# Chunk attention and a Mish feed-forward on one core: 72 transfers issued by GpSimd in place of SyncE

## The chip, the cores and the metric

The kernel runs on one core of a Trainium2 chip. The core has a matrix engine (TensorE, "PE" in the profile; its weight loads are shown apart as "PEld"), a vector engine (VectorE, "DVE"), an activation engine (ScalarE, "ACT"), GpSimd ("POOL") and SyncE ("SP"), which here issues transfers only. "SPq", "ACTq" and so on are the sequencers of these engines: what they do there (issue a transfer, wait for a semaphore) is not counted as busy time. Every engine works through its own list of instructions in order. Transfers run on 16 DMA engines that all issuing engines share.

The metric is the time of one execution on the device in microseconds (us); lower is better.

## What is computed

Inputs are q, k and v of shape 8 x 8 x 576 x 64 in float32 and two float64 weight matrices, `w_in` (512 x 2048) and `w_out` (2048 x 512).

```python
# attention in chunks of 64 positions, every head on its own
scores = q_c @ k_c.T / 8                 # 64 x 64 for each chunk
attn = softmax(scores)
x = (attn @ v_c)                         # as 4608 tokens x 512
# feed-forward
h = x @ w_in
g = h * tanh(softplus(h))                # Mish
out = g @ w_out
```

The result is 4608 x 512 in float32. The matrix products are made from float32 values split into an upper and a lower part, with three matmuls for each product.

## The kernel before

**Work and stages.** The tokens are worked on in 18 pairs of 256 tokens. Pairs 0 and 1 form the first block; the other 16 make four blocks of four pairs. While a block goes through the feed-forward, the attention of the next one is made beside it.

- *First block* (0 to about 138 us). It does three things at once: attention and feed-forward of pairs 0 and 1; the unpacking of the float64 weights, piece by piece (`w_load`, L102, loads a piece into the tile `wst`; `w_scale`, `w_bits`, `w_hi` and `w_lo` turn it into upper and lower parts in `wi` and `wo`; `w_bits` also stores `w_in`'s whole values to `cs` in DRAM, L136); and attention of pairs 2 to 5. The order of all steps on all engines is written out by hand in the string `ORDER`, and nothing is reordered afterwards (`tc.manual_schedule()`). Two pieces of weights fit into `wst`, so a load waits until `w_bits` is done with the piece two before it. `w_keep` ("keep", L169 and L170) stores `w_in`'s parts to `wa` in DRAM.
- *Blocks 1 and 2* (about 138 to 503 us). The product with `w_in` is made with seven half-size products in place of eight (`product`, L756), for which sums and differences of quarter blocks of the weights and of x are needed. A block takes eight steps `unit(m, u)`, each of seven products in the order of `PRODUCTS`, and then `phase_two(m)`. A product's weight operand is a tile `w` of 256 KB, loaded by `load_op` (L743) from `wa`; the load is put in the list five products ahead of its use. The first blocks of weights (A11, A12, A22) were stored by `w_keep`, the sums (S1 to S4) by `s_lo`.
- *Blocks 3 and 4* (about 503 to 838.8 us). Both products are made with seven half-size ones (`up_two`, `down_all`); `load_op` also loads from `wb`, where `t_keep` and `t_lo` put the parts of `w_out` and its sums.

**The sums of weights.** For each of eight parts u of `w_in`, `s_load(u)` (L184) loads the whole values from `cs` into the tile `a`; `s_adds` (L196, VectorE) makes four sums; `s_hi` (L200, ScalarE) and `s_lo` (L204, VectorE) split them; `s_lo` then stores them to `wa` (L207). There is one buffer for `a`, so `s_load(u + 1)` waits for that store to land. Parts 0 and 1 start in the first block, and part u is made during unit u - 1 of block 1, at the places in `S_PLACES`. For `w_out`, `t_whole`, `t_sums`, `t_hi` and `t_lo` do the same from `wo`, without a load, during block 2, and `t_lo` stores to `wb` (L237).

**q, k and v.** `load_qk` (L261) loads q and k of a pair and `load_v` (L269) its v, 512 KB each. Pairs 0 and 1 are loaded at the very start, into tiles named `q`, `k` and `room`. In the first block the pairs 2 to 5 take a tile `qk` from the pool `xo` of seven buffers, which also serves the two `room` tiles, the weights `wi` and the parts of x; later pairs take two buffers of the pool `at` (three buffers, shared with `p`, `ps` and `v`) or of `ob`. In the ORDER string the loads of the later pairs stand between steps of the weights, for example

```
... load 0, scale 0, ..., a_T 1 1, a_copy 1 1, a_V 1 1, load_qk 0, scores 0, ...
... hi 18, lo 18, s_load 0, inverse 3, x 0 8, up 14, fill 13, fill 14, norm 3, keep 5, load_v 3, keep 7, ...
... s_hi 0, s_lo 0, s_load 1, x 0 6, T 3, up 15, copy 3, ops 3, gl 14, fill 15, V 3, ...
```

(`load_qk 0` is pair 2, `load_v 3` pair 5.) In block 1 and 2 a unit loads v for the pair whose scores it makes and q and k for the next pair (`unit`, L816 to L841).

**Queues.** Nearly all transfers are issued by SyncE, in the order in which the steps are listed. An issue that has to wait for a semaphore (a buffer, data, or the landing of a transfer eight places back) holds all that follow on that engine. ScalarE issues two of the first loads of k and some of the last stores. GpSimd issues none: it sets four constants and the identity matrix at the start and has no further work.

Of the kernel before, what the change touches and what calls it, by code (L numbers as in the profile page):

```python
# [23 lines left out]
def kernel(  # L24
# [22 lines left out]
    nc = tc.nc  # L47
# [11 lines left out]
    at = ctx.enter_context(tc.tile_pool(name="at", bufs=3))  # L59
# [19 lines left out]
    ops_of = [dram.tile([P, 7, 2, 256], F32, name=f"wa_{u}") for u in range(NU)]  # L79
    ops_out = [dram.tile([P, 7, 2, 256], F32, name=f"wb_{u}") for u in range(NU)]  # L80
# [100 lines left out]
    def s_load(u):  # L181
        if u < NU:
            bld["t"] = c_p.tile([P, 4, 2, 256], F32, name=f"a_{u}", tag="c")
            nc.sync.dma_start(  # L184
                out=bld["t"][:, :, 1], in_=w_c[u].rearrange("p h (a c) -> p (h a) c", a=2)
            )

# [14 lines left out]
    def s_lo(u):  # L202
        t = bld["t"]
        nc.vector.tensor_tensor(  # L204
            out=t[:, :, 1].bitcast(F32R), in0=t[:, :, 1], in1=t[:, :, 0], op=ALU.subtract
        )
        nc.sync.dma_start(out=ops_of[u][:, 3:], in_=t)  # L207


    def t_whole(u):  # L210
# [21 lines left out]
    def t_lo(u):  # L232
        t = bld["o"]
        nc.vector.tensor_tensor(
            out=t[:, :, 1].bitcast(F32R), in0=t[:, :, 1], in1=t[:, :, 0], op=ALU.subtract
        )
        nc.sync.dma_start(out=ops_out[u][:, 3:], in_=t)  # L237

    def t_keep(u):
        for n, (f, a) in enumerate(((0, 0), (1, 0), (1, 1))):  # L240
# [6 lines left out]
    st = {}  # L247
    BOTH = slice(0, 2)

    def load_qk(j, qk=None, ts=(BOTH,), queues=(nc.sync, nc.sync), pool=(at, "A")):  # L250
        if qk is None:
            if pool[0] is xo_p:
                both = xo_p.tile([P, 2, 2, H, CHUNK], F32, name=f"qk_{j}", tag="x")
                qk = [both[:, 0], both[:, 1]]
            else:
                qk = [
                    pool[0].tile([P, 2, H, CHUNK], F32, name=f"{n}_{j}", tag=pool[1]) for n in "qk"
                ]
        for t in ts:
            for x, src, queue in zip(qk, (q, k), queues):  # L260
                queue.dma_start(  # L261
                    out=x[:, t], in_=src[2 * j : 2 * j + 2][t].rearrange("t p h c -> p t h c")
                )
        st[j] = {"q": qk[0], "k": qk[1]}

    def load_v(j, vs=None):
        if vs is None:
            vs = at.tile([P, 2, H, D], F32, name=f"v_{j}", tag="A")
        nc.sync.dma_start(out=vs, in_=v[2 * j : 2 * j + 2].rearrange("t p h c -> p t h c"))  # L269
        st[j]["v"] = vs  # L270

    def small_mm(o, l, r, ts):
# [126 lines left out]
    def first_pair(m):  # L399
        return PAIRS + 4 * (m - 1)  # L400
# [58 lines left out]
    def up(i, cols=slice(0, TOK), last="x"):  # L459
        x = xs["first"]  # L460
        if i not in it:
            it[i] = {"h": ps_h.tile([P, TOK], F32, name=f"h_{i}", tag="h")}
        h = it[i]["h"]
        n = 0
        parts = ((1, 0), (0, 0), (0, 1))
        for w_, x_ in parts if last == "x" else reversed(parts):
            for kt in range(NK):
                nc.tensor.matmul(  # L468
                    h[:, cols],
                    lhsT=wi[i // 2][:, i % 2 * 2 + kt // 2, w_, kt % 2],  # L470
                    rhs=x[:, x_, kt, cols],
                    start=(n == 0),
                    stop=(n == 3 * NK - 1),
                )
                n += 1
# [86 lines left out]
    FIRST, SECOND = slice(0, 1), slice(1, 2)  # L562
# [6 lines left out]
    A, B = slice(0, PTOK), slice(PTOK, TOK)  # L569
# [6 lines left out]
    def room(n):  # L576
        if n not in rooms:
            rooms[n] = xo_p.tile([P, 2, 2, H, CHUNK], F32, name=f"room_{n}", tag="x")
        return rooms[n]

    def open_accumulators():
        first.close()
        opened["o"] = ctx.enter_context(tc.tile_pool(name="ps_o", bufs=1, space=bass.MemoryType.PSUM))

    TOP = {
        "qk0": lambda: load_qk(0, None, (FIRST, SECOND), (nc.sync, nc.scalar)),
        "v0": lambda: load_v(0, room(0)[:, 0]),
        "qk1": lambda: load_qk(1, (room(0)[:, 1], room(1)[:, 0]), (FIRST, SECOND)),
        "v1": lambda: load_v(1, room(1)[:, 1]),
        "up0A": lambda: up(0, A),  # L590
        "up0B": lambda: up(0, B),
        "up1": lambda: up(1, last="w"),
# [52 lines left out]
    def atom(name, *args):  # L645
# [9 lines left out]
        elif name in steps:  # L655
            steps[name](a)
        elif name in attention:
            attention[name](j)
        elif name == "up":
            up(a, last="w")  # L660
        elif name == "gh":
            g_upper(it[a], it[a]["z"], f"0_{a}", a in BY_SCALAR)
        elif name == "gl":
            g_lower(it[a], it[a]["z"], f"0_{a}")
        elif name == "fill":
            if a < NF - 1:
                filled()
            down(0, a, it[a])
        elif name == "mish":
            it[a]["z"] = z_tile(f"z_{a}")  # L670
            mish(it[a]["z"], it[a]["h"])
        elif name == "keep":
            w_keep(a)
        elif name == "x":
            x_step(1, *args)
        elif name == "ops":
            for _ in range(a):
                load_op()
        else:
            {"s_load": s_load, "s_adds": s_adds, "s_hi": s_hi, "s_lo": s_lo}[name](a)  # L680

    attention = {
        "scores": a_scores,
        "load_v": load_v,
        "max": a_max,
        "sub": a_sub,
# [5 lines left out]
        "V": a_values,  # L692
        "raw": a_raw,
        "load_qk": lambda j: load_qk(j, pool=(xo_p, "x")),
    }

# [72 lines left out]

    zb = {}  # L770
    S_STEPS = (s_adds, s_adds, s_hi, s_lo, s_load)
    S_PLACES = ((1, 1, 1, 3, 5), (0, 3, 3, 4, 6), (2, 2, 4, 4, 6))
    X_LATE = ((9, 0), (10, 4), (6, 2), (8, 0))
# [8 lines left out]

    BUILDS_OUT = {}
    T_STEPS = (t_whole, t_sums, t_hi, t_lo)
    for n in range(NU):
        for i, step in enumerate(T_STEPS if n < NU - 1 else ()):
# [420 lines left out]
    with tc.manual_schedule():  # L1207
# [6 lines left out]
        p = first_pair(BOTH_FROM - 1)  # L1214
# [53 lines left out]
```

## Time and profile before

| | |
|---|---|
| Time, median of 3 runs | 843.26 us (843.57, 840.75, 843.26) |
| Time of the profiled execution | 840.62 us |
| Its span, first to last instruction | 838.8 us |
| TensorE busy | 804.2 us (96%) |
| VectorE, ScalarE, GpSimd busy | 529.9, 437.6 and 0.7 us |
| Bytes on the queue of SyncE | 179.60 MB, of 181.38 MB in all |
| Mean granted TensorE clock | 0.993 of full speed |

In rows of the profile, "L756 PE MATMUL x<-x_T,w" is line 756, the engine, the operation, and the tile written from the tiles read. In a list in order of time the first two numbers are start and duration in us, and "[2.56 <-DMA v<-in_v]" says that the engine stood idle for 2.56 us before and that the landing of v ended it. In a list of waits the three numbers are us in total, times, and the longest. "DMA wst<-in_w_in" in the chain of work that ended last is a transfer, from issue to landing. In the page's list of issues the last number is the median us from issue to landing. TensorE's clock is a share of full speed.

### The profile page before, as it was taken

How to read it: one execution, taken by the hardware profiler on the slowest of the kernel's cores; microseconds unless marked ns; L12 is line 12 of the kernel's file. 1: busy time of each engine (PE TensorE's matmuls, PEld its weight loads, DVE VectorE, ACT ScalarE, POOL GpSimd, SP SyncE). 2: the span in 40 equal slices, each digit the busy share in tenths (PEclk: the TensorE clock that was granted, in tenths of full speed). 3: DMA queues.
4: the chain of work that ended last, by engine and by line, in shares of the span. 5: the costliest groups of instructions: out<-in, count | busy, mean ns of one | idle time of the engine just before them, and what ended most of it. 6: DMA issues, size and time to landing. Idle time of an engine off the chain costs nothing.

```text
span 838.8 us, 15546 instructions
## 1 busy us (share of the span) xinstructions
PE 804.2 (96%) x6088; PEld 673.5 (80%) x6088; DVE 529.9 (63%) x797; ACT 437.6 (52%) x649; POOL 0.7 (0%) x6
## 2 busy tenths in 40 slices
PE   4889988899999999999999999999999999999998
PEld 3668776688888887788888888787899988888887
DVE  5988997646465654576574844554798723348875
ACT  4788884444354444354444535555656524445443
POOL 0000000000000000000000000000000000000000
PEclk9999999999999999999999999999999999999999
DMA  8799957875876403888876129876567786666763
GB/s 285 258 326 307 322 198 262 301 264 193 281 254 202 126 1 113 277 264 276 285 247 210 39 101 310 278 229 180 160 182 207 208 238 194 191 193 177 213 194 104
DMA packets 92280, 181.38 MB, mean 216 GB/s; under 512 B 9008, under 2 KB 23344, under 8 KB 90160
## 3 DMA queue, kind: packets, MB, share of 16 engines
q1 hardware_dynamic: 91600, 179.60, 67.7%
q8 instruction: 49, 0.80, 0.4%
q10 hardware_dynamic: 608, 0.79, 0.3%
q14 instruction: 23, 0.19, 0.1%
HBM read 137.36 MB, written 42.99 MB: 215 GB/s over the span
## 4 chain that ended last, share of the span: by engine, by line
PE 73%; DVE 10%; DMA 8%; ACT 5%; issue 2%; SPq 1%; DVEq 0%; ACTq 0%
PE x L756 17%; PE v L756 9%; PE y L756 5%; PE X L1115 4%; DMA wst<-in_w_in 4%; PE Z L1115 3%; PE Z L1067 3%; PE X L1067 2%; PE X_a L1067 2%; DVE wc L132 2%; PE av L278 2%; PE s L278 2%; PE Y L1067 1%; PE o_(1, 1)_0_2753 L506 1%; PE o_(2, 1)_0_4405 L506 1%
## 5 line engine op out<-in xcount | busy, mean ns | idle before, releaser
L756 PE MATMUL x<-x_T,w 128*128 128x512 f32 x576 | 144.6, 395 | 1.9 <-ACT G L1001 1.1
L756 PEld LDWEIGHTS x<-x_T,w 128*128 128x128 f32 x576 | 107.1, 189 | 27.4 <-ACT G L1001 2.8
L1021 ACT CAST gh<-G 128x512 fp32r<-128x512 f32 x96 | 59.1, 621 | 58.2 <-PE X_a L1067 16.3
L1023 DVE TENSOR_TENSOR gl<-G,gh 128x512 fp32r<-128x512 f32 x96 | 65.4, 690 | 29.3 <-ACT gh L1021 28.4
L481 ACT ACTIVATE G<-G 128x512 f32<-128x512 f32 x48 | 30.3, 632 | 57.4 <-DVE G L768 57.4
L768 DVE TENSOR_TENSOR G<-v,G 128x512 f32<-128x512 f32 x32 | 21.9, 690 | 57.1 <-ACT G L1001 34.7
L468 PE MATMUL h<-x_first,wi 128*128 128x512 f32 (+1 forms) x204 | 47.6, 383 | 4.1 <-ACT z L481 3.0
L756 PE MATMUL v<-x_T,w 128*128 128x512 f32 x192 | 48.0, 393 | 2.1 <-DMA w<-wa 2.1
L756 PE MATMUL y<-x_B,w 128*128 128x512 f32 x192 | 49.0, 398 | 0.3 <-DMA w<-wa 0.3
L481 ACT ACTIVATE zb<-zb 128x512 f32<-128x512 f32 x32 | 20.2, 632 | 55.6 <-DVE zb L768 55.5
L756 PE MATMUL v<-x_B,w 128*128 128x512 f32 x192 | 48.5, 393 | 0.0
L756 PE MATMUL x<-x_B,w 128*128 128x512 f32 x192 | 48.2, 393 | 0.0
L468 PEld LDWEIGHTS h<-x_first,wi 128*128 128x128 f32 x204 | 36.1, 188 | 12.9 <-ACT z L481 3.8
L756 PEld LDWEIGHTS v<-x_T,w 128*128 128x128 f32 x192 | 36.0, 188 | 10.2 <-DVE a L196 2.5
L492 DVE CAST gh<-z 128x512 fp32r<-128x512 f32 x39 | 16.5, 424 | 41.0 <-PE o_(2, 0)_3_3320 L506 20.6
L756 PEld LDWEIGHTS v<-x_B,w 128*128 128x128 f32 x192 | 35.7, 188 | 7.9 <-DVE zb L768 0.4
L506 PE MATMUL o<-wo,gh 128*128 128x512 f32 x128 | 40.7, 398 | 1.0 <-DVE wo L160 1.0
L756 PEld LDWEIGHTS y<-x_B,w 128*128 128x128 f32 x192 | 35.1, 188 | 8.0 <-issue 0.4
L756 PEld LDWEIGHTS x<-x_B,w 128*128 128x128 f32 x192 | 35.4, 188 | 7.1 <-issue 0.2
L1115 PE MATMUL X<-w,gh 128*128 128x256 f32 x256 | 36.0, 284 | 0.0
L496 DVE TENSOR_TENSOR gl<-z,gh 128x512 fp32r<-128x512 f32 x48 | 32.9, 690 | 1.3
L1115 PEld LDWEIGHTS X<-w,gh 128*128 128x128 f32 x256 | 33.1, 192 | 0.1
(211 smaller groups left out, 1673.4 us busy)
## 6 DMA issues: line engine op xcount, KB each, us to landing
w<-wa SPq DMA_DIRECT2D x224, 256.0 KB, 3.2
w<-wb SPq DMA_DIRECT2D x112, 256.0 KB, 2.9
v<-in_v SPq DMA_DIRECT2D x16, 512.0 KB, 5.8
wa<-a SPq DMA_DIRECT2D x8, 1024.0 KB, 4.9
wb<-t SPq DMA_DIRECT2D x8, 1024.0 KB, 5.0
wst<-in_w_out SPq DMA_DIRECT2D x7, 1024.0 KB, 7.1
wst<-in_w_in SPq DMA_DIRECT2D x6, 1024.0 KB, 7.9
q<-in_q SPq DMA_DIRECT2D x12, 512.0 KB, 4.3
```

The source lines that it names most:

```text
L132: nc.vector.scalar_tensor_tensor(out=c, in0=x, scalar=mask, in1=y, op0=op, op1=ALU.bitwise_or)
L278: nc.tensor.matmul(o[h * CHUNK : (h + 1) * CHUNK, c, t - ts.start, g], lhsT=l[rows, t, 2 * g + h], rhs=r[rows, t, 2 * g + h], start=True, ...
L468: nc.tensor.matmul(h[:, cols], lhsT=wi[i // 2][:, i % 2 * 2 + kt // 2, w_, kt % 2], rhs=x[:, x_, kt, cols], start=(n == 0), stop=(n == 3 * ...
L481: nc.scalar.activation(out=out_, in_=in_, func=AF.Mish)
L496: nc.vector.tensor_tensor(out=d["gl"], in0=z, in1=d["gh"].bitcast(F32), op=ALU.subtract)
L506: nc.tensor.matmul(acc[t], lhsT=g[:, t * P : (t + 1) * P], rhs=wo[:, f, part], start=(f == 0 and n == 0), stop=(f == NF - 1 and n == 2),)
L756: nc.tensor.matmul(o, lhsT=t[:, w_, kt], rhs=x[x_][:, kt], start=(start and i == 0), stop=(i == 5), skip_group_check=not start,)
L768: nc.vector.tensor_tensor(out=z, in0=o, in1=z, op=ALU.add)
L1021: nc.scalar.copy(out=d["gh"], in_=g)
L1023: nc.vector.tensor_tensor(out=d["gl"], in0=g, in1=d["gh"].bitcast(F32), op=ALU.subtract)
L1067: nc.tensor.matmul(o, lhsT=d[g][:, t * P : (t + 1) * P], rhs=w__, start=(first and n == 2), stop=(u == NU - 1 and g == "gl"), skip_group_c ...
L1115: nc.tensor.matmul(o, lhsT=d[g][:, t * P : (t + 1) * P], rhs=w_[:, part], start=(k in (0, 1, 3) and u == 0 and t % 2 == 0 and n == 0), sto ...
```

## The change

`load_qk` and `load_v` issue from GpSimd unless told otherwise; the first two pairs are told to use SyncE (and ScalarE for pair 0's k), as before. `s_load`, and the stores in `s_lo` and `t_lo`, issue from GpSimd. All other transfers, among them the weight loads `w_load` and `load_op`, the stores `w_keep`, `t_keep` and those of the output, stay where they were. No buffer, size or step is changed, nor the order in which the steps are listed.

```diff
     def s_load(u):
...
-            nc.sync.dma_start(
+            nc.gpsimd.dma_start(
                 out=bld["t"][:, :, 1], in_=w_c[u].rearrange("p h (a c) -> p (h a) c", a=2)
             )
...
     def s_lo(u):
...
-        nc.sync.dma_start(out=ops_of[u][:, 3:], in_=t)
+        nc.gpsimd.dma_start(out=ops_of[u][:, 3:], in_=t)
...
     def t_lo(u):
...
-        nc.sync.dma_start(out=ops_out[u][:, 3:], in_=t)
+        nc.gpsimd.dma_start(out=ops_out[u][:, 3:], in_=t)
...
-    def load_qk(j, qk=None, ts=(BOTH,), queues=(nc.sync, nc.sync), pool=(at, "A")):
+    def load_qk(j, qk=None, ts=(BOTH,), queues=(nc.gpsimd, nc.gpsimd), pool=(at, "A")):
...
-    def load_v(j, vs=None):
+    def load_v(j, vs=None, queue=nc.gpsimd):
...
-        nc.sync.dma_start(out=vs, in_=v[2 * j : 2 * j + 2].rearrange("t p h c -> p t h c"))
+        queue.dma_start(out=vs, in_=v[2 * j : 2 * j + 2].rearrange("t p h c -> p t h c"))
...
         "qk0": lambda: load_qk(0, None, (FIRST, SECOND), (nc.sync, nc.scalar)),
-        "v0": lambda: load_v(0, room(0)[:, 0]),
-        "qk1": lambda: load_qk(1, (room(0)[:, 1], room(1)[:, 0]), (FIRST, SECOND)),
-        "v1": lambda: load_v(1, room(1)[:, 1]),
+        "v0": lambda: load_v(0, room(0)[:, 0], nc.sync),
+        "qk1": lambda: load_qk(1, (room(0)[:, 1], room(1)[:, 0]), (FIRST, SECOND), (nc.sync, nc.sync)),
+        "v1": lambda: load_v(1, room(1)[:, 1], nc.sync),
```

## The prediction

> **What bounds the kernel now.** I read the page first (span, busy shares), then the busy time by stage: the stretch and its length, busy us (and instructions) of PE, PEld, DVE, ACT and POOL, then the granted clock, the DMA engines' busy share and GB/s.
>
> ```profile
> span 838.8 us, 15546 instructions
> PE 804.2 (96%) x6088; PEld 673.5 (80%) x6088; DVE 529.9 (63%) x797; ACT 437.6 (52%) x649; POOL 0.7 (0%) x6
> ```
> ```profile
> 0.00:40.00 40.00, 24.36 (x395) 19.96 (x396) 30.65 (x52) 23.48 (x37) 0.70 (x6) 0.96 0.79 265
> 40.00:165.00 125.00, 113.10 (x961) 89.44 (x960) 103.73 (x131) 91.21 (x110) 0.00 (x0) 0.98 0.83 286
> 165.00:503.00 338.00, 337.41 (x2385) 276.69 (x2384) 197.57 (x298) 153.23 (x221) 0.00 (x0) 1.00 0.61 197
> 503.00:750.00 247.00, 245.35 (x1874) 214.60 (x1873) 132.76 (x200) 127.97 (x205) 0.00 (x0) 1.00 0.72 214
> ```
>
> TensorE is idle 838.8 - 804.2 = 34.6 us. Of that, 15.6 us lie before 40 us, 11.9 us between 40 and 165 us, 2.2 us between 165 and 750 us, and the other 4.9 us after that, where none of the moved transfers is issued. From 165 us on TensorE is full, so a transfer there can cost time but hardly win any. What can be won lies in the first block and in the two units after it, up to 165 us.
>
> **What is moved.** The page's list of issues holds all of it:
>
> ```profile
> v<-in_v SPq DMA_DIRECT2D x16, 512.0 KB, 5.8
> wa<-a SPq DMA_DIRECT2D x8, 1024.0 KB, 4.9
> wb<-t SPq DMA_DIRECT2D x8, 1024.0 KB, 5.0
> q<-in_q SPq DMA_DIRECT2D x12, 512.0 KB, 4.3
> k<-in_k SPq DMA_DIRECT2D x12, 512.0 KB, 6.2
> a<-cs SPq DMA_DIRECT2D x8, 512.0 KB, 5.3
> qk<-in_q SPq DMA_DIRECT2D x4, 512.0 KB, 7.8
> qk<-in_k SPq DMA_DIRECT2D x4, 512.0 KB, 8.4
> out<-C SPq DMA_DIRECT2D x4, 64.0 KB, 2.0
> ```
>
> That is 16 + 8 + 8 + 12 + 12 + 8 + 4 + 4 = 72 transfers (the last row is only a yardstick). Their bytes and their number stay. What changes is their place: on SyncE each waits until everything listed before it has been issued; on GpSimd, which has nothing else to do after its start, each goes when its own buffer is free, behind the other moved ones only. Weight loads and stores on SyncE no longer stand behind them.
>
> No row shows a GpSimd transfer, so its issue time x is bounded: below by SyncE's 0.32 us for the store of sums, above by the 2.0 us that a short transfer takes from issue to landing. I take 1.0 us: two to three times the 0.32 to 0.54 us of the nearest rows.
>
> **1. The start, +2.7 us.** Pair 2's q and k go out on SyncE only at 17.77 us, behind weight loads. Their tile is the fourth taken from a pool of seven, so it has never been used and waits for nothing: on GpSimd they go at about 1.3 us, when its last set-up instruction ends.
>
> ```profile
> 1.01 0.29 POOL masks.py:199 TENSOR_SCALAR_AFFINE_SELECT ident<-ident 128x128 f32<-128x128 f32 x1
> 17.77 0.44 SPq L261 DMA_DIRECT2D qk<-in_q  x1
> 3.00:12.80 9.80, 3.36 (x68) 2.67 (x68) 5.81 (x12) 1.26 (x3) 0.00 (x0) 1.00 1.03 385
> 12.76 0.67 ACT L114 ACTIVATE wc<-wst 128x512 f32<-128x512 f32 x1 [2.84 <-DMA wst<-in_w_in]
> ```
>
> From 3.0 to 12.8 us the DMA engines are full (share 1.03, 385 GB/s), and ScalarE waits at the end of it for the first weights. Another 1.05 MB is 1.05 / 0.385 = 2.7 us. ScalarE's in-order queue holds the first block's next copies behind this load, and VectorE's bit work on these weights follows it, so I pass it on whole. Bounds: 0 if GpSimd's first transfers only get going after 12.8 us; 2.7 at most.
>
> **2. 25 to 130 us: +1.0, then 1.6 back.** Pair 2's v waits for the transposes of pair 1; pair 3's q and k then wait for nothing.
>
> ```profile
> 24.39 0.93 PE L346 MATMUL pt<-ident,p 128*128 128x128 f32 x4
> 28.88 6.20 DMA wst<-in_w_in
> 28.00:32.00 4.00, 3.62 (x50) 3.12 (x45) 3.93 (x8) 3.97 (x7) 0.00 (x0) 0.99 0.90 287
> 54.22 0.82 SPq L261 DMA_DIRECT2D qk<-in_q  x1
> ```
>
> So 1.57 MB leave their places (pair 3's q stood at 54.22) and go at 25.3 + 2.7 = 28 us, just ahead of the load of 28.88 (then 31.6), which the chain names. At 287 GB/s some 1.0 MB is gone by 31.6, and the other 0.55 MB would hold the load up by at most 1.9 us. I take the middle, 1.0; bounds 0, and 1.57 / 0.287 = 5.5 if all of it goes first. In return the weight loads after 54 us run without 1.05 MB of q and k (2.7 us at 385 GB/s), so the weight chain is about even by its end; TensorE's own order keeps the lag of 3.7 us except where it now waits for something on time:
>
> ```profile
> PE h L468 <- DVE wi L160: 0.6, 1, 0.6
> PE o L506 <- DVE gl L496: 1.7, 2, 1.0
> ```
>
> 0.6 and the 1.0 can be absorbed, leaving 2.1 us of lag at 130 us.
>
> **3. The last v of the block, -2.1 us.** SyncE stands 12.2 us at the first load for the sums, until VectorE has split the last weights, with two pairs of stores and pair 5's v behind it.
>
> ```profile
> SPq L184 <- DVE wo L160: 12.2, 1, 12.2
> 124.85 8.26 DMA v<-in_v
> 130.20 1.00 ACT L356 COPY ps<-pt 128x1024 f32<-128x1024 f32 x1
> 133.25 1.51 PE L278 MATMUL av<-ps,v 64*64 64x64 f32 x64 [2.56 <-DMA v<-in_v]
> 132.00:140.00 8.00, 6.75 (x82) 5.57 (x82) 5.26 (x10) 3.30 (x6) 0.00 (x0) 0.79 0.47 176
> ```
>
> The stores will go out during those 12.2 us. The v stays behind the load of sums, now on GpSimd, but shares the DMA engines with much less: instead of 8.26 us it should land in about the median 5.8, near 130 us, and the scores' copy is done by 131.2. TensorE, ready at 133.25 - 2.56 = 130.7 and lagging 2.1, starts at 132.8: 0.45 us sooner, with no wait. After the wait of 2.56 the granted clock is 0.79 over 8 us, a loss of 8 x 0.21 = 1.7 us. Without the wait I expect none. Together -2.1; bounds 0 (the copy comes late, since it stands behind the split of the sums on ScalarE) and -2.56 - 1.7 = -4.3.
>
> **4. Unit 1, ending at -1.6 us.** What is late next is the second store of sums and the weight loads that read it.
>
> ```profile
> 148.07 7.53 DMA wa<-a
> 158.51 0.59 SPq L184 DMA_DIRECT2D a<-cs  x1
> 159.14 4.21 DMA w<-wa
> 163.49 1.97 PE v L756 x6
> ```
>
> The store starts 0.45 us sooner and takes 0.7 longer to issue (1.0 against 0.32). It took 7.53 us where the median of its kind is 4.9, beside pair 6's q and k, which go earlier on GpSimd: half of the 2.6 us, 1.3, is my estimate (bounds 0 and 2.6). The load of sums ahead of the weights leaves SyncE: -0.6. Sum -0.45 + 0.7 - 1.3 - 0.6 = -1.65 at 163 us. TensorE, 2.1 ahead, waits there instead: the gain beyond 1.65 is eaten. From here TensorE is full, and the rest keeps this.
>
> **5. Units up to 258 us, 0.** A sums tile has one buffer: load, adds, split, store, and only then the next load.
>
> ```profile
> 208.02 0.80 SPq L743 DMA_DIRECT2D w<-wa  x2
> 208.87 0.54 SPq L184 DMA_DIRECT2D a<-cs  x1
> 214.85 1.80 DVE L196 TENSOR_TENSOR a<-a 128x256 f32<-128x256 f32 x4 [2.70 <-DMA a<-cs]
> 219.07 0.32 SPq L207 DMA_DIRECT2D wa<-a  x1
> 219.74 0.59 ACT L862 COPY zb<-x 128x512 f32<-128x512 f32 x1 [1.95 <-PE x L756]
> ```
>
> Two issues become longer by x - 0.32 each, and the load no longer stands behind two weight loads (208.02 to 208.87, 0.85): 2 x 0.68 - 0.85 = +0.5 us for the adds. ScalarE, whose copy TensorE needs next, has 1.95 us to spare after the split. That cover hides it. Without it, 0.5 us in each of the three units that wait in this way. The loads of q, k and v and the stores of w_out's sums are queued a unit or a phase before their use and land in 4 to 6 us; on GpSimd they stand behind at most one store and one load of sums, so I cost them at nothing.
>
> **The sum.** -1.6 us on the profiled 840.62 us (span 838.8 and 1.8 around it) is 839.0. The three runs have a median of 843.26, 2.6 above the profiled one. On that basis: 841.7 us. About 0.3%, 2.5 us, is what a measurement of this kernel can tell from no change.
>
> **Rivals.** *No effect, 843.3 us:* the order on SyncE was holding nothing that counts, and only its issue time goes: some 72 x 0.44 us = 32 us of an engine that no path runs through for long. Then the early transfers wait in the DMA engines instead of in SyncE's list, which the full share of 1.03 allows; against it stand the 12.2 us of step 3, in which SyncE held transfers back while the chain went on to them. The Trainium skill, DMA: Bandwidth & Descriptors, "Issuing engines are not separate DMA queues", has this as its rule: transfers issued from several engines share the same 16 DMA engines, and spreading them saves only the sequencer's issue time. The full share agrees with the first half of the rule; by the second half the sum would be 0 instead of -1.6.
>
> *Faster, 838.3 us:* step 1 costs little, because GpSimd's first transfers come late or VectorE has room; then step 3 gives its 4.3, step 4 the full 2.6, and the wait at 163 us with its clock loss shrinks too: between -2.6 and -6.8; I take -5. In numbers: -2.56 + 0.7 - 2.6 - 0.6 = -5.1 and a like clock loss of 1.7, estimated as after the other wait. For it: the waits it removes are in the rows. Against it: share 1.03 at the start.
>
> *Slower, 846.3 us, the early transfers crowd the weights:* GpSimd pulls each q, k and v forward into a full DMA stretch, the 5.5 us of step 2 come whole, and TensorE lags 2.7 + 5.5 - 1.6 = 6.6 us at 130.7: the v product starts at 137.3, +4.0, its clock loss of 1.7 is saved, but the second store follows the +4.0; step 4's other terms leave +2.8, or +4.1 without the 1.3. I take +3.0. It decides from a lag of about 6 us. Against it: the bytes taken forward are missing later.
>
> ```profile
> L492 DVE CAST gh<-z 128x512 fp32r<-128x512 f32 x39 | 16.5, 424 | 41.0 <-PE o_(2, 0)_3_3320 L506 20.6 <-PE o_(1, 0)_3_1664 L506 18.9 <-ACT z L481 1.4
> ```
>
> *Slower, 846.0 us, GpSimd's own issue:* from x = 1.72 on, 2 (x - 0.32) - 0.85 exceeds the 1.95 us of cover. At x = 2.0 and one 0.42 us cast of VectorE in the way the excess is 1.0 us, three times; step 3 then gives nothing and step 4 leaves 1.7 - 1.3 - 0.6 = -0.2: about +2.8. Against it: x would be twice my estimate. The Trainium skill (SBUF — State Buffer, "SBUF: two separate sides") warns that VectorE's two-port fast modes lock GpSimd out while it writes descriptors. No row here shows that; by it x would grow while such a cast runs.
>
> **Chances.** My forecast 0.31 and no effect 0.11, which make one result (own range 840.7 to 845.8), faster 0.33, crowding 0.13, GpSimd's issue 0.12. So faster by over 0.3%: 0.33, within: 0.42, slower: 0.25. The range runs from the best case, 843.3 - 6.8 = 836.5, to 847.0, a little beyond the slower cases' +2.8.
>
> **What would show it.** Step 1: the first weights' scaling at about 15.5 instead of 12.76 us, and pair 2's q and k issued by GpSimd before 4 us. Step 2: the chain's load of 28.88 issued near 31.6 and landing in about 7 us. Step 3: the stores of the last operands between 111 and 122 us, the v product near 132.8 with no wait for v, and a granted clock of 1.00 after it. Step 4: TensorE at the v product of unit 1 near 161.8. Step 5: the adds waiting near 3.2 us and TensorE full. I am wrong if the first weights land no later, if TensorE shows idle time between 165 and 503 us, or if a GpSimd issue is far from 1 us.

## Result, and the profile after

The changed kernel takes 847.97 us (median of 10 runs, 844.34 to 851.72), the kernel before 840.95 (10 runs, 838.69 to 843.57): ratio 1.0081, 95% interval 1.0057 to 1.0106, some 7 us slower. Ratios here leave out disturbed executions, so they can differ a little from the quotient of the medians. The profiled execution of after is the slowest of its ten (851.72 us), so places are read from its trace, and sizes from medians.

The page and the busy time by stage, as before: stretch, busy us (instructions) of PE, PEld, DVE, ACT, POOL, then granted clock, DMA share, GB/s.

```profile
span 850.0 us, 15603 instructions
PE 805.5 (95%) x6088; PEld 673.6 (79%) x6088; DVE 529.9 (62%) x797; ACT 437.0 (51%) x649; POOL 50.3 (6%) x78
```
```profile
0.00:40.00 40.00, 22.02 (x382) 18.51 (x383) 27.85 (x49) 20.15 (x33) 4.41 (x11) 1.00 0.76 270
40.00:165.00 125.00, 111.43 (x958) 87.45 (x958) 102.31 (x127) 90.35 (x110) 10.56 (x15) 1.00 0.77 272
165.00:503.00 338.00, 332.80 (x2356) 272.06 (x2355) 199.25 (x301) 154.41 (x221) 28.83 (x43) 0.99 0.61 201
503.00:750.00 247.00, 244.34 (x1869) 213.66 (x1868) 132.01 (x198) 126.65 (x202) 6.49 (x9) 1.00 0.71 208
```

GpSimd has its 72 transfers, and TensorE does the same work. From 165 to 503 us, where it had 337.41 us of work in 338, it now has 332.80: the idle time has reached a stage that was full. GpSimd's issues in order of time show when the transfers now go:

```profile
1.45 0.84 POOL L261 DMA_DIRECT2D qk<-in_q  x1
2.28 0.72 POOL L261 DMA_DIRECT2D qk<-in_k  x1
29.00 0.72 POOL L269 DMA_DIRECT2D v<-in_v  x1 [25.99 <-PE pt L346]
29.71 0.72 POOL L261 DMA_DIRECT2D qk<-in_q  x1
30.43 0.72 POOL L261 DMA_DIRECT2D qk<-in_k  x1
64.77 0.73 POOL L269 DMA_DIRECT2D v<-in_v  x1 [33.61 <-ACT gh L490]
...
91.92 0.72 POOL L269 DMA_DIRECT2D v<-in_v  x1 [24.99 <-PE pt L346]
```

Each v pulls the next pair's q and k along, 1.57 MB in 2.2 us, at 29, 65 and 92 us. The chain that ended last passes through weight loads that are issued 1.3 to 6.6 us behind these triples (31.77, 72.00 and 99.96) and land in some 10 us (start, us from issue to landing):

```profile
5.93 9.70 DMA wst<-in_w_in
...
31.77 10.11 DMA wst<-in_w_in
...
47.07 6.68 DMA wst<-in_w_in
...
72.00 9.80 DMA wst<-in_w_in
...
99.96 9.69 DMA wst<-in_w_in
...
115.70 1.06 PE pt L346 x8
...
163.83 6.36 DMA w<-wa
```

Before, the load of 28.88 landed in 6.20 us. The DMA part of 27 to 42 us in after shows what the load of 31.77 met: queues with packets, MB and share of the engines' time (q1 is SyncE's, q0 GpSimd's), then transfers, KB each, median us to landing.

```profile
q1 hardware_dynamic: 991, 2.95, 59.5%
q0 software_dynamic: 432, 1.57, 26.2%
...
wst<-in_w_in SPq DMA_DIRECT2D x1, 1024.0 KB, 10.1
...
v<-in_v POOLq DMA_DIRECT2D x1, 512.0 KB, 6.0
qk<-in_q POOLq DMA_DIRECT2D x1, 512.0 KB, 9.0
qk<-in_k POOLq DMA_DIRECT2D x1, 512.0 KB, 11.0
```

GpSimd's k, issued at 30.43, lands at 41.4; the weights, issued 1.3 us later, at 31.77 + 10.11 = 41.9. The two queues share the engines for ten microseconds and end together. The Trainium skill, DMA: Bandwidth & Descriptors, "Queues, rings and completion order", says that each DMA engine goes round between the queues that have work, a packet at a time; these two landings agree with it. The moved bytes also travel in other pieces than before: SyncE's queue had 91,600 packets and now has 72,016, so 19,584 left it, while GpSimd's queue has 10,368, for the same 46.14 MB. Whether larger packets win GpSimd's queue a larger share, no run here tells.

TensorE in after, at the places of the steps:

```profile
139.21 1.16 PE L278 MATMUL av<-ps,v 64*64 64x64 f32 x64 [0.26 <-ACT ps L356]
170.33 2.90 PE L756 MATMUL v<-x_T,w 128*128 128x512 f32 x6 [3.00 <-DMA w<-wa]
355.29 1.66 PE L756 MATMUL v<-x_T,w 128*128 128x512 f32 x6 [1.58 <-DVE z L768]
523.01 1.61 PE L756 MATMUL x<-x_T,w 128*128 128x512 f32 x6 [0.94 <-ACT G L999]
```

The last v of the block no longer makes TensorE wait (0.26 us, before 2.56), but it stands 5.96 us later (139.21 against 133.25). The wait for weights at unit 1's v product grew from 2.13 to 3.00, and two waits are new. The first of them goes back to VectorE's first sum of w_out's parts, which waits for the last store of the first output block; before, and after:

```profile
341.74 1.23 DVE L217 TENSOR_TENSOR t<-wo 128x1024 f32<-128x1024 f32 x1 [3.51 <-DMA out<-ob_1b]
```
```profile
351.77 1.23 DVE L217 TENSOR_TENSOR t<-wo 128x1024 f32<-128x1024 f32 x1 [5.45 <-DMA out<-ob_1b]
```

### The profile page after: what moved, and what is told of

Read it like the earlier page. It is cut to its first block, busy times and chain, and to the rows that moved or that the text cites. A ratio compares the mean times of both kernels' runs of the same rounds, so it can differ in the third digit from the quotient of the medians.

```text
span 850.0 us, 15603 instructions
## 1 busy us (share of the span) xinstructions
PE 805.5 (95%) x6088; PEld 673.6 (79%) x6088; DVE 529.9 (62%) x797; ACT 437.0 (51%) x649; POOL 50.3 (6%) x78
## 3 DMA queue, kind: packets, MB, share of 16 engines
q1 hardware_dynamic: 72016, 133.46, 51.1%
q0 software_dynamic: 10368, 46.14, 15.3%
## 4 chain that ended last, share of the span: by engine, by line
PE 73%; DMA 10%; DVE 8%; ACT 5%; issue 4%; POOL 0%; SPq 0%; DVEq 0%; ACTq 0%; POOLq 0%
PE x L756 18%; PE v L756 9%; DMA wst<-in_w_in 6%; PE y L756 5%; PE X L1115 4%; PE Z L1115 3%; PE Z L1067 3%; PE X L1067 2%; PE X_a L1067 2%; PE s L278 2%; PE av L278 2%; PE o_(1, 0)_0_1593 L506 1%; PE Y L1067 1%; PE o_(1, 1)_0_2753 L506 1%; DVE wc L132 1%
## 5 line engine op out<-in xcount | busy, mean ns | idle before, releaser
L492 DVE CAST gh<-z 128x512 fp32r<-128x512 f32 x39 | 16.7, 428 | 42.1 <-PE o_(2, 0)_3_3320 L506 20.6
L768 DVE TENSOR_TENSOR zb<-v,zb 128x512 f32<-128x512 f32 x32 | 21.9, 685 | 20.3 <-ACT zb L862 20.3
```

What stands on the lines that cost most here:

```text
L492: nc.vector.tensor_copy(out=d["gh"], in_=z)
L768: nc.vector.tensor_tensor(out=z, in0=o, in1=z, op=ALU.add)
```

## Experiments

Theory T: the transfers cost through their time. SyncE's list had held them back; on GpSimd they go as soon as their buffers are free, beside transfers that are needed sooner. Rival I: GpSimd as issuer costs (longer issues, an in-order queue of its own). A ratio is to runs of the kernel before beside it, whose medians lie between 840.66 and 841.88; gains and losses in us below are against those. "Late" compares the start of the same matmul in two traces. Such a lag is good to about 2 us: kernels that issue alike up to 110 us differ in it by up to 2.2 us at 113 (the loads for the sums alone on GpSimd, against the kernel before).

| Kernel | us | ratio, 95% interval |
|---|---|---|
| all 72 on GpSimd (the change) | 847.97 | 1.0081, 1.0057 to 1.0106 |
| first block's q, k, v back on SyncE | 843.18 | 1.0024, 0.9999 to 1.0049 |
| first block's q, k, v alone on GpSimd | 845.35 | 1.0047, 1.0029 to 1.0064 |
| sums alone on GpSimd | 839.23 | 0.9974, 0.9955 to 0.9993 |
| the change, pair 2's q, k back | 846.35 | 1.0053, 1.0026 to 1.0081 |
| all on GpSimd, held back (first try) | 853.72 | 1.0148, 1.0116 to 1.0180 |
| sums on GpSimd, pair 2's q, k early on SyncE | 842.81 | 1.0029, 1.0008 to 1.0049 |
| first block back, the rest held back | 844.97 | 1.0040, 1.0020 to 1.0061 |
| loads for the sums alone on GpSimd | 841.21 | 1.0001, 0.9980 to 1.0022 |
| stores of w_in's sums alone on GpSimd | 842.20 | 1.0016, 1.0000 to 1.0032 |
| all on GpSimd, first block held back | 842.80 | 1.0030, 1.0015 to 1.0046 |
| the same, late ones held back too | 840.88 | 1.0000, 0.9981 to 1.0019 |
| the same, pair 6's q, k on SyncE | 843.25 | 1.0012, 0.9996 to 1.0028 |
| the same, units' q, k, v on SyncE | 840.73 | 1.0006, 0.9986 to 1.0027 |
| the same, only units' v on SyncE | 838.60 | 0.9963, 0.9940 to 0.9986 |

**Halves of the change.** First block's pairs back on SyncE:

```diff
-        "load_v": load_v,
+        "load_v": lambda j: load_v(j, queue=nc.sync),
-        "load_qk": lambda j: load_qk(j, pool=(xo_p, "x")),
+        "load_qk": lambda j: load_qk(j, queues=(nc.sync, nc.sync), pool=(xo_p, "x")),
```

> The changed kernel with pairs 2 to 5 of the first block (their q, k and v) back on SyncE; the sums and all later q, k and v stay on GpSimd. Crowding theory (the early transfers of the first block go ahead of weight loads): the lag of 6 to 7 us that the changed kernel has at the v product of unit 1 (170.33 instead of 163.49) goes, first weights scaled near 12.8 us, and the gain at the last v of the block stays, since SyncE no longer stands 12.2 us: 836 to 841 us. Rival (GpSimd as issuer costs in the units, where the changed kernel lost another 4 us after 168 us: 1.6 at 345 and 1.2 at 512): still 843 to 846 us, with these stalls in the trace. Third (nothing but transfers being off SyncE matters): 848 us as the changed kernel.

843.18 us: 1.4 us over the kernel before where the change has 7.0, but at the foot of what the rival expected (843 to 846, with the stalls in the trace) and not the 836 to 841 of the crowding theory. The lag at unit 1's v product is 1.1 us instead of 6.8, but the two late stalls are there, and the gain at the last v (132.14 instead of 133.25) is lost by then. So the early transfers of the first block make most of the lag, and what the two stalls come from is open. TensorE, late in this run:

```profile
346.07 1.67 PE L756 MATMUL v<-x_T,w 128*128 128x512 f32 x6 [0.94 <-DVE z L768]
```
```profile
513.75 1.62 PE L756 MATMUL x<-x_T,w 128*128 128x512 f32 x6 [0.89 <-DMA w<-wa]
```

The complement, with the defaults of `load_qk`, `load_v`, `s_load`, `s_lo` and `t_lo` back at `nc.sync` and the two lambdas above given `nc.gpsimd`:

> The complement: only q, k and v of pairs 2 to 5 of the first block on GpSimd, everything else on SyncE as before. Crowding theory: the lag of the first block comes whole and the wait for the last v goes as well, since that v no longer stands behind the load of sums: 845 to 849 us, TensorE 5 to 8 us late at the v product of unit 1. Rival (the units carry the loss): 840 to 842 us, no lag left at 165 us.

845.35 us, as T expects. Unit 1's v product is 4.6 us late (168.10; expected were 5 to 8), and the late stalls are absent. Sums alone (the defaults of `load_qk` and `load_v` at `nc.sync`):

> Only the loads and stores of the sums on GpSimd, all q, k and v on SyncE. Crowding theory: nothing goes forward in the first block, SyncE no longer stands 12.2 us at the first load for the sums, so the wait of 2.56 us for the last v and the clock loss of 1.7 us behind it shrink: 837 to 840 us. If that wait does not carry on to the end: 841 us. Rival (loads and stores of sums on GpSimd are late and hold the units): 843 to 845 us.

839.23 us, faster, as T expects. TensorE starts the last v product without waiting for v, and unit 1's v product waits 0.48 us (before 2.13), without the clock loss behind it; the window has a granted clock of 1.00, where before had 0.81 and after 0.78:

```profile
132.13 1.16 PE L278 MATMUL av<-ps,v 64*64 64x64 f32 x64 [0.34 <-ACT ps L356]
...
161.75 1.61 PE L756 MATMUL v<-x_T,w 128*128 128x512 f32 x6 [0.48 <-DMA w<-wa]
...
202.86 1.64 PE L756 MATMUL v<-x_B,w 128*128 128x512 f32 x6 [1.09 <-DVE zb L768]
```
```profile
165.00:173.00 8.00, 8.00 (x41) 6.71 (x40) 4.95 (x8) 4.05 (x6) 0.53 (x1) 1.00 0.51 197
```

At 168 us it is 3.35 us ahead of before; 1.5 of that is given back by 206, the larger part at the row of 202.86, which had no wait in before: TensorE runs into the sums' chain. Pair 2's q and k back:

```diff
+            j, queues=(nc.sync if j == PAIRS else nc.gpsimd,) * 2, pool=(xo_p, "x")
```

> The changed kernel with only pair 2's q and k (the two transfers issued at 1.45 and 2.28 us) back on SyncE. If the start term of 2.9 us is passed on whole: 845 us, the first weights scaled near 12.8 us, every weight load up to 107 us about 2.9 us sooner. Rival (the triples at 29, 65 and 92 us set the lag by themselves, and the start is absorbed in their waits): 847 to 848 us. A third way: more than the start is won, since the first triple then no longer meets a late weight load: 842 to 844 us.

846.35 us, 4.6 over the kernel before instead of 7.0, between the first two readings; its interval overlaps that of the change, so the start's share is some 2 us or none. Its trace has the first weights at 12.81 us and TensorE on time at 40, but 4.5 us late at 107: the triples make that lag without the start.

**Time or issuer.** A small GpSimd copy of a value written at about the wanted moment holds each load back on the same queue:

```diff
+    tick = const.tile([P, 1], F32, name="tick")
+    def hold(x):
+        while len(x.shape) > 2:
+            x = x[:, 0]
+        nc.gpsimd.tensor_copy(out=tick, in_=x[:, 0:1])
...
+            hold(a1["z"])
             load_v(j)
```

> The changed kernel with GpSimd still issuing all 72 transfers, but each q, k and v of the first block, of the units and of the down phases held back by one small GpSimd copy of a value that is written at about the time at which SyncE issued that transfer in the kernel before (pair 2's q and k at 17 to 19 us instead of 1.45; pair 3's at 54 instead of 29.71; the q at 346 behind the mish of its unit). If it is the earlier time that costs, and not the issuer: as with the sums alone on GpSimd, 838 to 841 us, no lag at the v product of unit 1, no stall at 345 and 512 us. If GpSimd as issuer costs (longer issue, its own in-order queue): still 845 to 848 us.

853.72 us: worse, and no verdict on I, since one hold was ill chosen. (In the kernels with holds the lines below them stand 7 or more lower: L268 is L261, L276 is L269.) The value for pair 2 came at 27.30 us, not near 17:

```profile
27.30 0.67 POOL L255 COPY tick<-ps 128x1 f32<-128x1 f32 x1 [25.99 <-ACT ps L363]
27.91 0.84 POOL L268 DMA_DIRECT2D qk<-in_q  x1
```

TensorE was 10 us late from 30 us on. The opposite test puts pair 2's q and k early on SyncE, with the sums on GpSimd (`load_qk 0` leaves its later place in the list):

```diff
-        rooms, qk0, v0, a_scores 0 0, ...
+        rooms, qk0, v0, early, a_scores 0 0, ...
+        "early": lambda: load_qk(PAIRS, both["qk"]),
```

> Only the sums on GpSimd, all q, k and v on SyncE, but pair 2's q and k stand early in SyncE's list, behind the first pair's v (issued near 2.5 us instead of 17.3; their tile is set aside first, so no buffer changes). If the early time costs whoever issues it: the first weights are scaled near 15.5 us, TensorE is 2.6 us later at 30 to 40 us than with the sums alone on GpSimd, and of this 1.5 to 3 us reach the end: 841 to 842 us. If only GpSimd's second queue lets a transfer push in: 839 us, first weights near 12.8 to 13.5 us.

842.81 us, a little over what T expected, and some 4 us more than the sums alone; the intervals are apart. ScalarE's first weights come as late as in the change, with no GpSimd queue in it:

```profile
15.64 0.66 ACT L114 ACTIVATE wc<-wst 128x512 f32<-128x512 f32 x1 [5.54 <-DMA wst<-in_w_in]
```

For the start, then, the place in time costs, whoever issues. On SyncE part of the cost comes another way: the first weight load is itself issued only at 7.59 us (5.73 with the sums alone), behind two more transfers of its own list, and lands in 8.03 us (6.89). First block on SyncE and the later ones held back:

> As the run with the first block's q, k and v back on SyncE (843.2 us), with the later ones on GpSimd held back as above. If its two stalls (TensorE waits 0.94 us at 346, behind VectorE's first whole weight that waits for the last store of the output; 0.89 us at 514 for weights behind q and k issued at 505) come from q and k that go beside those stores and loads: both go, 839 to 841 us. If they come from GpSimd as issuer: 843 us, both stalls still there.

844.97 us, a miss with two parts. Both late stalls are gone, as T expects; but one new hold put q and k of pair 6 right ahead of the second store of sums:

```profile
146.72 0.71 POOL L268 DMA_DIRECT2D q<-in_q  x1 [0.40 <-issue]
147.42 0.73 POOL L268 DMA_DIRECT2D k<-in_k  x1
148.13 0.58 POOL L207 DMA_DIRECT2D wa<-a  x1
158.73 0.76 POOL L184 DMA_DIRECT2D a<-cs  x1 [10.02 <-DMA wa<-a]
```

The store needs 10.3 us, and TensorE loses 4.5 us between 150 and 164 us. This looks like the same mechanism, made by hand; no run takes that one hold away from this kernel. Holds with better values (pair 2's is the low part of the first weights), in the first block alone:

```diff
+        ("load_qk", 0): lambda: wi[0][:, 0, 1, 0].bitcast(F32),
+        ("load_v", 0): lambda: wc[7]["c"].bitcast(F32),
+        ("load_qk", 1): lambda: st[2]["r", 0],
...
+        if name in ("load_qk", "load_v") and (name, a) in WHEN:
+            hold(WHEN[name, a]())
```

> The changed kernel, GpSimd issuing all 72 transfers, with only the first block's q, k and v held back to about the times at which SyncE issued them before; pair 2's q and k now wait for the low part of the first weights (about 17.7 us; in the earlier held run their hold came at 27.3 us, and TensorE was 10 us late from there on). If the early time makes the first block's loss: about the run with those transfers back on SyncE, 842 to 844 us, first weights scaled near 12.8 us, no lag beyond 1 us at 107 us. If GpSimd as issuer makes it: 847 to 849 us.

842.80 us, as T expects, and against I for the first block: the same queue and the same issues, 5 us less, the interval apart from that of the change. TensorE is 0.4 us late at 107 instead of 8.2. The late stalls remain (0.56 us at 345, 0.99 at 513). With the late ones held as well:

```diff
+            if m > 1: hold(a1["z"])
             load_v(j)
...
+                    hold(G[units[1], "G11"])
                     load_qk(j + 1, pool=(ob_p, "ob"))
```

> As the run before it, and the q, k and v from the second block on held back as well, but not those of the units before 258 us, where the earlier hold put q and k right ahead of a store of sums (it landed after 10.31 us). If the stalls at 345 and 512 us come from q and k that go early: 2.2 us less than the run before it, 839.5 to 841.5 us, both stalls gone. If from the issuer: the same time as the run before it, 842 to 844 us.

840.88 us, inside what was expected, and no different from the kernel before; both stalls are gone. (The interval still touches that of the run before it, so the 1.9 us rest on the traces as well.) Between 502 and 514 us the stores of the output (median us to landing) show what the second stall met. With q and k of the next pair issued at 505.04 and 505.75 (first block back on SyncE), and held to 512.39 (here):

```profile
out<-ob_2b SPq DMA_DIRECT2D x8, 128.0 KB, 4.7
```
```profile
out<-ob_2b SPq DMA_DIRECT2D x8, 128.0 KB, 2.4
```

Before it was 2.3. So beside two early 512 KB loads eight 128 KB stores take twice as long to land, and the weights listed behind those come late.

**Which of the sums' transfers win.** `s_load` alone, and the store in `s_lo` alone, on GpSimd:

> Only the 8 loads for the sums on GpSimd; the stores of sums and all q, k and v on SyncE. If the gain of the sums' transfers is that SyncE no longer stands 12.2 us at the first such load: 838.5 to 840 us, all of the gain of the run with the sums alone (839.2). If the stores of sums off SyncE carry a part: 840 to 842 us.

> Only the 8 stores of w_in's sums on GpSimd; their loads, w_out's stores and all q, k and v on SyncE. SyncE stands 12.2 us at the first load for the sums as before, so the last v of the block comes late and its wait of 2.56 us stays: if that standing is what the sums' transfers win, 841 us, no gain. If the stores carry the gain (the loads alone gave none, ratio 1.0001): 838.5 to 840 us. If it takes both together: 841 us here too, and only the run with both wins.

841.21 and 842.20 us: neither wins alone. With the stores alone SyncE still stands at the load, as expected:

```profile
SPq L184 <- DVE wo L160: 12.8, 1, 12.8
```

With the loads alone the last v product starts without waiting for v, so that part of the reading was right, but the second load of sums lands in 8.1 us instead of 6.2 (with all the sums there) and unit 0 loses it again. That this is the rule, and not that execution, is not shown. The stores of w_out's sums alone on GpSimd were not run; in the trace of the sums alone the lead is the same before their first store as at the end (1.9 and 2.0 us).

**The rest.** Held back, all 72 give 840.88 us; the sums alone 839.23. Pair 6's q and k on SyncE:

> As the run with the first block's and the late transfers held back (840.9 us, no different from the kernel before, where the sums alone on GpSimd gave 839.2), but pair 6's q and k, which GpSimd issued at 138.0 and 138.7 us beside the weights of unit 0 and ahead of the second store of sums, are back on SyncE (about 143.5 us there). If these two are what is left between the two runs (1.6 us at the v product of unit 1 in their traces): 838.5 to 840 us. If something else, such as the holds themselves or GpSimd as issuer: 840.5 to 842 us.

843.25 us, not won. In its trace GpSimd issues pair 6's v right behind a load of sums, ahead of unit 1's weights, and TensorE waits for them:

```profile
157.46 0.71 POOL L276 DMA_DIRECT2D v<-in_v  x1
```
```profile
166.38 2.90 PE L775 MATMUL v<-x_T,w 128*128 128x512 f32 x6 [4.60 <-DMA w<-wa]
```

So all q, k and v of the units before 258 us, and then their v alone, went back to SyncE:

> As the run with the first block's and the late transfers held back, with every q, k and v of the units before 258 us back on SyncE; the held ones and the sums stay on GpSimd. If the transfers of these units, put ahead of the units' weights, make the rest of the difference: 838.5 to 840 us, as the sums alone; TensorE's wait for weights at the v product of unit 1 below 1 us. If GpSimd as issuer or the holds make it: 840.5 to 842 us.

> The same with only the v of these units back on SyncE, their q and k on GpSimd. If it is the v that goes ahead of unit 1's weights (issued right behind the load of sums; 157.46 us against 159.15 for the weights): 838.5 to 840 us, the v product of unit 1 waits less than 1 us. If not: 840.5 to 843 us, as with them on GpSimd.

840.73 and 838.60 us. Only the v back is the fastest kernel here, 0.9963 (0.9940 to 0.9986), faster than before and not distinguishable from the sums alone. But all of them back give no gain (0.9986 to 1.0027), which by what was expected points to the holds or to GpSimd as issuer, and speaks against a simple account by the v; and at unit 1's v product TensorE still waits 1.66 us in the one trace (put down to the sums' adds) and 2.12 in the other (for weights), where less than 1 was expected. What makes the last 2 us stays open, and rival I is not ruled out for them.

## Why the prediction was wrong

Predicted were 841.7 us and no measurable change; 847.97 came, beyond the range's 847.0. The mechanism of the rival "the early transfers crowd the weights" (846.3, chance 0.13) is what happened, but that its time comes near is in part luck: it stood for +3.0 us, where +7.0 was measured, and its basis of 843.26, from three runs, was 2.3 us above the median of ten.

*Step 1, right.* First weights scaled at 15.65 (forecast 15.5; before 12.76), the loss passed on whole: 2.9 us for 2.7.

*Step 2 failed, and with it the sum.* It let the lag go from 2.7 to 2.1 us by 130 us; it went from 2.9 to 8.2 (the transposition that stood at 107.50 stands at 115.70; this execution is 3.75 us above the median). Its bounds of 0 to 5.5 were for one triple. I costed the triple ahead of the load of 28.88 at 1.0 us, where the lag grew by 2.5, put the two later triples at nothing, where it grew by 1.8 and 1.2 (each within the 2 us named above, their sum is not), and gave 1.6 back because "the bytes taken forward are missing later". They are missing for one load: that of 47.07 lands in 6.68 us, its counterpart of 40.30 before in 8.26. But TensorE won nothing back by it, and every v sets off the next q and k, so the loads of 72.00 and 99.96 met triples as well. Landing times of all of the block's weight loads (min, median, max), before and after:

```profile
DMA to landing us min/median/max: 4.3/7.2/8.4
```
```profile
DMA to landing us min/median/max: 4.3/7.8/10.7
```

The lag was 5.0 us at 47 us, 5.2 at 82, 7.0 from 83 and 8.2 from 107 (times of the kernel before): it came in steps and nothing was won back between them. Held back, the same transfers on the same queue cost 5 us less in the medians, so it is shown that their early time makes this loss.

*Step 3, right in mechanism, its clock term too large.* The stores went out in SyncE's standing time (116.70 to 121.21 us), the v product waits 0.26 us, and the clock is full behind it (133 to 141 us in after, granted clock 1.00):

```profile
133.00:141.00 8.00, 7.35 (x96) 5.94 (x95) 6.53 (x12) 4.07 (x6) 0.57 (x1) 1.00 0.37 139
```

The lag falls by 2.3 us at the v product (forecast: from 2.1 to -0.45, so 2.55). But the full clock adds only 1.1 us by 138, not 1.7, and TensorE's next wait takes 0.8 of that back by 141 (lag 5.97, 4.89 and 5.64 where the kernel before stands at 133.25, 138.05 and 140.97). The 1.7 counted all of the 8 us, of which TensorE worked 6.75; 6.75 x 0.21 is 1.4. The sums alone show the same numbers without the crowding: 2.2, 1.1 and 0.7. That the standing alone is what the sums win is not borne out: the loads alone gave nothing.

*Step 4 failed in the change, held for the sums alone.* From 141 to 172 us the forecast gave back 0.5 us (from 2.1 ahead to 1.65); the sums alone gained 1.9, the change lost 2.4. The sums alone start unit 1's v product at 161.75, as forecast (161.8), and win 1.6 more behind it, where the clock stays full, which the sum had left out. In the change the store landed in 6.3 us as I had estimated (7.53 less 1.3), but the weights of 163.83 come behind v (161.89), TensorE waits 3.00 us for them, and the clock is 0.78 over the next 8 us:

```profile
165.00:173.00 8.00, 5.00 (x17) 3.75 (x16) 7.36 (x12) 4.26 (x5) 0.10 (x1) 0.78 0.79 295
```

*Step 5, right for the change, but its last sentence failed.* From 172 to 258 us nothing is lost in the change, which comes 8 us late; the sums alone, which come early, give back 1.5 us at 206. And GpSimd's issues are no bound: ns min, median and max of one, x was 0.57 us for the stores and 0.72 for v (I took 1.0), well below 1.72.

```profile
L269 POOL DMA_DIRECT2D v<-in_v x16: 704/717/727, 29.0 to 578.7; - x16
```
```profile
L207 POOL DMA_DIRECT2D wa<-a x8: 572/572/575, 139.8 to 260.4; - x8
```

So rival "GpSimd's own issue" falls. The rule on VectorE's fast modes (the Trainium skill, SBUF — State Buffer, "SBUF: two separate sides") would stretch x while such a cast runs. Ten of the 72 issues overlap a cast of VectorE (L492), and they took 0.57 to 0.75 us like the rest, so no longer x is seen here; one cast, begun 0.39 us into an issue, took 0.58 us, where none of the kernel before took over 0.43. The loads of q, k and v in the later units I cost "at nothing", because they themselves come in time. Who is behind them I did not ask: 1.9 us by 350 and 1.2 at 523 in the trace, 1.9 in the medians (842.80 to 840.88).

The medians add up roughly: sums -2.5 us, early q, k and v of the first block +5 (3.6 where they alone move), of the late units +2, and some +2.5 that no run places, in the units between, the holds or the issuer: +7.

Moving a transfer to another list thus changed when it starts, and for the early q, k and v that was worth some +7 us, far more than their issue time. The rule that spreading transfers over issuing engines saves only issue time (the Trainium skill, DMA: Bandwidth & Descriptors, "Issuing engines are not separate DMA queues") held as to the engines, which are shared, but "only" did not: it left out that the order in an issuing engine's list is also what holds a transfer back.

## What to carry to other kernels

An in-order issue list is also a schedule: before moving a load off it, ask not only whether the load still comes in time, but what it will now go ahead of, and go on asking for each load that the first one sets off. Move the transfers that block the list while they wait (here the sums, whose first load stood 12.2 us; loads and stores won only together), and leave the ones that are early anyway, or hold them back with a small instruction on the new queue that reads a value written at the right moment, after a look at when that value really comes.

## What the hardware showed

A plain transfer of 512 KB occupies GpSimd for 0.70 to 0.84 us, against a median of 0.435 us for v on SyncE in the kernel before (row at the end, ns), alike whether VectorE was working (48 of the 72 issues) or not. In the one stretch looked at, two queues did not take turns by transfer: a 1 MB load on one, issued 1.3 to 2.8 us behind 1.57 MB on the other, ended 0.5 us after the last of them. And beside two 512 KB loads the landing time of 128 KB stores doubled, from 2.3 to 4.7 us, in a stage where the engines' mean share was only 0.61 to 0.72.

```profile
L269 SPq DMA_DIRECT2D v<-in_v x16: 383/435/1282, 46.2 to 576.4; - x16
```
